# Turning transposed sums back to rows on GpSimd instead of ScalarE, with earlier row and weight loads, in a transformer block kernel

## The chip, the core and the metric

The kernel runs on one core of a Trainium2 chip. Its time is the device time of one execution in microseconds (us), and the median of several runs is given. A core has engines that work side by side, each through its own list of instructions in order: PE (TensorE, matrix products), DVE (VectorE), ACT (ScalarE), POOL (GpSimd) and SP (SyncE, which here only issues transfers). PEld is the weight load that belongs to a product and overlaps it. An instruction that waits for another engine or for a transfer holds up everything behind it in its own list.

## The reference, cut to what matters

One transformer block over 2048 rows of width 512, all in float32: a LayerNorm with scale and shift from a condition vector, attention of 32 heads (8 key and value heads, head size 128) over the last 512 cached keys, a gated residual, a second such LayerNorm, and a gated feed-forward part of width 1792 with its own gated residual.

```
mod = (silu(c) @ w_mod).reshape(1, 6, 1, 512);  sa, ca, ga, sb, cb, gb = mod
h = layernorm(x) * (1 + ca) + sa
x = x + ga * (softmax((h @ wq) @ k[-512:].T / sqrt(128)) @ v[-512:] @ wo)     # per head, k and v shared by 4 heads
h = layernorm(x) * (1 + cb) + sb
out = x + gb * ((gelu(h @ w_gate) * (h @ w_up)) @ w_down)
```

## The kernel before, in words

**Products.** Every float32 matrix is split into a high and a low float16 half, and `mm3` (line 90) makes each product out of three matmuls of 128x128 by 128x512 that accumulate in PSUM. A square of blocks is multiplied with seven block products instead of eight (`PROD`, numbered 1 to 7, with sums of blocks as operands); the partial results sit in chains named a, b and c.

**Stages.** The attention fills about the first 1340 us; its order is written out by hand for all engines. Then comes the feed-forward part, which the change touches. It is a loop over q = 0 to 27, with seven steps k = 0 to 6 in each, one block product per step. q counts pairs: n = q // 2 is a pair of 128-wide slices of the feed-forward width (seven pairs, `NP` = 7), and q even is the gate product, q odd the up product. The seven pairs are run twice, for the two halves g = 0 and g = 1 of the rows (n = 0 to 6 and n = 7 to 13). For g = 1 the LayerNorm rows must be prepared during g = 0: `ln_turned` loads a row tile, normalizes it on ACT (line 539), splits it into halves `xh` (lines 543 and 544) and has it transposed by a DMA (`xt`, line 549); `turned_out` (lines 558 and 559) makes scaled float32 tiles `hf`, which go to DRAM; `combos` loads them again (`cb`) and makes the block sums.

**Down product.** For the first five pairs of each half (`turned(n)`), the product with w_down is made transposed with the seven-product scheme. `yt_add` (lines 1657 and 1660) gathers it on DVE in eight tiles `yt`, one for each c of four column blocks and qb of two groups of 512 rows. For the last two pairs (`NROW` = 2) the product is made directly as rows, `y_tasks` (line 952), and added to the row tiles `acc`, eight of them for a half. After the fifth pair the eight `yt` tiles are turned back to rows, in four steps. `yt_turn` splits the 32-bit words of a tile into two 16-bit halves (`yu`, line 1666, on ACT); a DMA transposes them as 16-bit data (`yv`, line 1671, issued by SP); the rows of y1, the residual, are loaded into `acc` (`load_acc`, line 96); and `yt_row` puts the two halves together again for one row tile (`yr`, line 1686, on ACT, which reads pairs of 16-bit values that lie 1 KB apart) and adds the result to `acc` (line 1687, on POOL). `f_final` writes a row tile to the output when its three contributions are in.

**Order.** In the feed-forward part the list of SP is in program order; those of PE, ACT, DVE and POOL are arranged by a planner that goes by estimated readiness. `f_at(q, k, fn)` puts a step at a place of the loop, `put_off(n, fn)` puts it n steps on. `wd_fetch` fetches row weights `wo`, `set_fetch` the gate and up weights `w` and `x`. Tiles share buffers by tag: `qt` has 3, `v16` 2, `raw` 5, `acc` 8, and `rw` and `wr` 2 each, which only the preparation of weights uses, earlier on.

Of the kernel before, what the change touches and what calls it, by code (L numbers as in the profile page):

```python
# [22 lines left out]
KT = D // P  # L23
NF = F // P
NT = S // P
QB = 512
QT = QB // P
# [18 lines left out]
NRW = 2  # L46
NWR = 2
NROW = 2
# [16 lines left out]
def block_kernel(ctx: ExitStack, tc: tile.TileContext, x, kT, v, wq, wo, wg, wu, wd, cT, wc, wm, out):  # L65
    nc = tc.nc

    const = ctx.enter_context(tc.tile_pool(name="const", bufs=1))
    pool = ctx.enter_context(tc.tile_pool(name="pool", bufs=2))
# [7 lines left out]
    def raw(name):  # L77
        return pool.tile([P, 512], F32, tag="raw", name=name, bufs=NRAW)
# [13 lines left out]
    acc, moved, bg = {}, [0], []  # L92

    def dma(out_, in_):
        moved[0] += 1
        nc.sync.dma_start(out_, in_)

    def load_acc(i, src, eng=None):
        acc[i] = pool.tile([P, D], F32, tag="acc", name="acc", bufs=2 * QT)
        (eng.dma_start if eng else dma)(acc[i], src)  # L100

    def rows_of(t, i):
        return t[i * P:(i + 1) * P, :]
# [3 lines left out]
    for i in range(QT):  # L107
        load_acc(i, rows_of(x, i), nc.scalar if i < 2 else None)
# [184 lines left out]
    def turned(n):  # L293

        return n % NP < NP - NROW
# [59 lines left out]
    BK, hs, y1 = {}, {}, {}  # L355

    def spilled(gen, key):
        if (gen, key) not in hs:
            n = KT if key in (0, 1) else 2
            hs[gen, key] = dram.tile([P, n, QB], F32, name=f"hs{gen}_{key}")  # L360
        return hs[gen, key]
# [94 lines left out]
    def put_off(n, fn):  # L456

        waits_.append([n, fn])
# [70 lines left out]
    def ln_turned(i):  # L529

        qb, i_ = divmod(i, QT)
        st = {}

        def load():
            st["x"] = raw("xs")
            dma(st["x"], y1[2 * QT + i])

        def norm():
            nc.scalar.activation(st["x"], st["x"], AF.Identity, bias=col("kinv", i), scale=col("kmax", i))

        def split():
            st["p"] = t = pool.tile([P, 2, W], F16, tag="p16", name="xh", bufs=NP16)
            nc.scalar.activation(t[:, 0, :], st["x"], AF.Copy)
            nc.gpsimd.tensor_tensor(t[:, 1, :], st["x"], t[:, 0, :], op=ALU.subtract)

        def turn():
            if i_ == 0:
                TURN[qb] = pool.tile([P, QT, 2 * KT, P], F16, tag="pt", name="xt", bufs=NPT)
            nc.sync.dma_start_transpose(TURN[qb][:, i_], st["p"].rearrange("p a b -> p (a b)"))

        return load, norm, split, turn

    def turned_out(qb, dt):
        tag, n = (("qt", 3), ("v16", 2))[dt % 2]
        f = pool.tile([P, D], F32, tag=tag, name="hf", bufs=n)
        v = f.rearrange("p (t q) -> p t q", t=QT)
        sc = cols[:, 4, dt:dt + 1]
        nc.scalar.activation(v, TURN[qb][:, :, dt, :], AF.Identity, scale=sc, bias=cols[:, 3, dt:dt + 1])
        nc.vector.scalar_tensor_tensor(v, TURN[qb][:, :, KT + dt, :], sc, v, op0=ALU.mult, op1=ALU.add)
        put_off(3, lambda: dma(spilled(3, qb)[:, dt, :], f))  # L560
# [170 lines left out]
    def at(key, *fns):  # L731
        later.setdefault(key, []).extend(fns)
# [300 lines left out]
    for i in range(QT, 2 * QT):  # L1033
        load_acc(i, rows_of(x, i))
# [175 lines left out]
    for g in range(NG):  # L1210
# [9 lines left out]
        elif g >= GW and (not half or pr < GW):  # L1220
            sched_set(g, srcs, t0, by, spread)
            if not half:
                a, b, c, d, e, f = SETPOS2 if g == GW else SETPOS
# [28 lines left out]
    NP = NF // 2  # L1252
# [283 lines left out]
    with tc.manual_schedule():  # L1536
        begin()
        nexty, invs = [], {}
        for t in range(T + TAIL):
            now[0] = t  # L1540
            u, s = divmod(t, 4)
# [70 lines left out]
    def f_at(q, k, *fns):  # L1612
        at(("f", q, k), *fns)

    for n in range(1, 2 * NP):
        for k, at_ in ((0, 1), (2, 3), (1, 4), (3, 5)) if turned(n) else ((0, 1), (1, 4)):
            f_at(2 * n + 1, at_, lambda n=n, k=k: wd_fetch(n, k))
    for q in range(3, NQ):
        for k, at_ in ((0, 2), (3, 2), (1, 3), (2, 4)):
# [2 lines left out]
    def step(q, fn):  # L1622
        f_at(q // 7, q % 7, fn)

    for i in range(2 * QT):
        q = 7 * (2 + i // 2) + 3 * (i % 2)
        load, norm, split, turn = ln_turned(i)
        step(q - 4, load)
        step(q, norm)
        step(q + 1, split)  # L1630
        step(q + 3, turn)
    for k, (qb, dt) in enumerate(((0, 0), (0, 2), (0, 1), (0, 3), (1, 0), (1, 2), (1, 1), (1, 3))):
        step(31 + 2 * k if k < 4 else 39 + k, lambda qb=qb, dt=dt: turned_out(qb, dt))
    for p in range(2):
        q = 51 + 14 * p
        for load, steps in combos(3, p, nc.gpsimd):
            step(q - 2, load)
            for off, fn in steps:
                step(q + 2 * off, fn)

    def f_final(ti):
        assert ti in back
        halfway[ti] = halfway.get(ti, 0) + 1
        if halfway[ti] <= NROW:
            return
        if ti >= 2 * QT:
            dma(rows_of(out, ti), acc[ti])
        else:
            put_off(2, lambda: dma(rows_of(out, ti), acc[ti]))

    YT, YR, back, halfway = {}, {}, set(), {}

    def yt_add(n, c, qb, ps):
        by = ST["dyc"][:, KT * (n % NP) + c:KT * (n % NP) + c + 1]
# [3 lines left out]
        else:  # L1658
            YT[key] = pool.tile([P, QB], F32, tag="acc", name="yt", bufs=2 * QT)
            nc.vector.tensor_scalar(YT[key], ps, by, None, op0=ALU.mult)  # L1660

    def yt_turn(g, c, qb):

        def split():
            u = YR["u", c, qb] = pool.tile([P, 2, QB], U16, tag="qt", name="yu", bufs=3)
            nc.scalar.activation(u, YT[g, c, qb].bitcast(U16).rearrange("p (r h) -> p h r", h=2), AF.Copy)

        def turn():
            if ("t", qb) not in YR:
                YR["t", qb] = pool.tile([P, KT, 2 * QT, P], U16, tag="pt", name="yv", bufs=NPT)  # L1670
            nc.sync.dma_start_transpose(YR["t", qb][:, c], YR.pop(("u", c, qb)).rearrange("p a b -> p (a b)"))

        split()
        put_off(3, turn)
        YR["n"] = YR.get("n", 0) + 1
        if YR["n"] % QT == 0:
            for i in range(QT):
                ti = 2 * QT * g + (YR["n"] - 1) % (2 * QT) // QT * QT + i
                put_off(3, lambda ti=ti: load_acc(ti, y1[ti]) or back.add(ti))

    def yt_row(g, qb, i):
        t = YR["t", qb].rearrange("p c (h i) q -> p c q h i", h=2)
        ti = 2 * QT * g + QT * qb + i
        assert ti in back
        r = raw("yr")
        nc.scalar.activation(r.bitcast(U16).rearrange("p (c q h) -> p c q h", c=KT, h=2), t[:, :, :, :, i], AF.Copy)
        nc.gpsimd.tensor_tensor(acc[ti], acc[ti], r, op=ALU.add)
        f_final(ti)
        if i == QT - 1:
            del YR["t", qb]  # L1690

    ADDS = {1: ((0, 0),), 2: ((0, 0),), 6: ((0, 1),), 5: ((1, 1),), 7: ((1, 1),), 4: ((1, 0),), 3: ((0, 1),)}
    YORDER = (1, 2, 6, 5, 7, 3, 4)
    LAST = {2: (0, 0), 7: (1, 1), 3: (0, 1), 4: (1, 0)}

    def yt_tasks(n):
        tasks = []
        for p in range(2):
            st = {}
            bk = banks(st, {"a": ("acc", "ya", NACC) if p else ("qa", "ya", 1), "b": ("acc", "yb", NACC), "c": ("acc", "yc", NACC)})  # L1700

            def group(k, p=p, bk=bk):
                a, b = PROD[k]
                x, start = CHAIN[k]
                ci, off = YCOL[a]
                w, t = WO["f", n, ci], A[n, {"b11": "11", "b21": "21", "b22": "22"}.get(b, b)]
                sl = slice(off + p * P, off + (p + 1) * P)
                mm3(bk(x)(), w[:, 0, sl], w[:, 1, sl], t[:, 0, :], t[:, 1, :], start, k in (2, 4, 3), True)

            def post(k, p=p, st=st):  # L1710
                (i, qb), = ADDS[k]
                yt_add(n, 2 * i + p, qb, st[CHAIN[k][0]])
                if n % NP == NP - NROW - 1 and k in LAST:
                    i, qb = LAST[k]
                    c, g = 2 * i + p, n // NP
                    put_off(2 if k in (3, 4) and p == k // 4 else 1, lambda: yt_turn(g, c, qb))
                    if p and k in (3, 4):
                        for r in range(QT):
                            put_off((9 if k == 4 else 13) + r, lambda r=r: yt_row(g, qb, r))

            tasks += [(lambda k=k, f=group: f(k), lambda k=k, f=post: f(k)) for k in YORDER]
        return [tasks[k:k + 2] for k in range(0, len(tasks), 2)]

    YCOL = {"a11": (0, 0), "a12": (0, 256), "s2": (1, 0), "s3": (1, 256), "s4": (2, 0), "s1": (2, 256), "a22": (3, 0)}
# [2 lines left out]
    for q in range(NQ):  # L1727
        n, m = divmod(q, 2)
# [55 lines left out]
```

## Time and profile before

| | |
|---|---|
| median of 3 runs | 1743.84 us (1743.32 to 1745.21) |
| the profiled execution's own time | 1743.57 us |
| its span, first to last instruction | 1741.8 us |
| PE busy | 1714.7 us, 98% |
| DVE busy | 1417.6 us, 81% |
| ACT busy | 1258.5 us, 72% |
| POOL busy | 1045.9 us, 60% |
| granted TensorE clock | 1.000 |

The profile's times count from the first instruction. PE's busy time counts the modelled end of each matmul, so a steady stream of matmuls shows as fully busy; how many were issued in a stretch tells more. A row of the timeline gives the start, the duration, the engine, line and operation, and in square brackets the idle time of the engine ahead of it with what ended it. A q behind an engine's name means its issuing part alone.

### The profile page before, as it was taken

How to read it: one execution, taken by the hardware profiler on the slowest of the kernel's cores; microseconds unless marked ns; L12 is line 12 of the kernel's file. 1: busy time of each engine (PE TensorE's matmuls, PEld its weight loads, DVE VectorE, ACT ScalarE, POOL GpSimd, SP SyncE). 2: the span in 40 equal slices, each digit the busy share in tenths (PEclk: the TensorE clock that was granted, in tenths of full speed). 3: DMA queues.
4: the chain of work that ended last, by engine and by line, in shares of the span. 5: the costliest groups of instructions: out<-in, count | busy, mean ns of one | idle time of the engine just before them, and what ended most of it. 6: DMA issues, size and time to landing. Idle time of an engine off the chain costs nothing.

```text
span 1741.8 us, 26188 instructions
## 1 busy us (share of the span) xinstructions
PE 1714.7 (98%) x8022; PEld 787.0 (45%) x8022; DVE 1417.6 (81%) x2454; ACT 1258.5 (72%) x2813; POOL 1045.9 (60%) x1266
## 2 busy tenths in 40 slices
PE   7999999999999999999999999999999999999998
PEld 5444444444444444444444444444444444444443
DVE  7898898888888899888888788888886678556674
ACT  6988788888878777898778778787784554643344
POOL 4889778776788884654675665754621558313422
PEclk9999999999999999999999999999999999999999
DMA  7999999999999999999999999899986663743235
GB/s 236 218 205 211 213 214 207 223 206 221 215 217 228 205 205 187 212 213 230 201 219 224 208 223 220 186 235 218 197 180 150 187 177 128 191 139 100 91 97 167
DMA packets 690636, 339.82 MB, mean 195 GB/s; under 512 B 578880, under 2 KB 601408, under 8 KB 690496
## 3 DMA queue, kind: packets, MB, share of 16 engines
q1 hardware_dynamic: 690208, 337.63, 85.5%
q8 instruction: 63, 1.03, 0.3%
q14 instruction: 77, 0.63, 0.1%
q10 hardware_dynamic: 288, 0.52, 0.1%
HBM read 135.66 MB, written 61.87 MB: 113 GB/s over the span
## 4 chain that ended last, share of the span: by engine, by line
PE 82%; ACT 5%; DVE 5%; DMA 3%; POOL 2%; issue 2%; SPq 0%; ACTq 0%; DVEq 0%; POOLq 0%
PE py L90 19%; PE ps L90 17%; PE po L90 17%; PE qa L90 8%; PE fa L90 6%; PE qc L90 4%; PE fc L90 3%; PE ya L90 2%; PE qb L90 2%; PE fb L90 2%; PE yc L90 1%; ACT ee L991 1%; DMA yv<-yu 1%; ACT p L1003 1%; DVE nm L982 1%
## 5 line engine op out<-in xcount | busy, mean ns | idle before, releaser
L991 ACT ACTIVATE ee<-ps,nm 128x512 f32<-128x512 f32 x512 | 350.1, 684 | 191.9 <-DVE nm L982 189.3
L1008 DVE SCALAR_TENSOR_TENSOR p<-ee,rr,p 128x512 f16<-128x512 f32 x512 | 460.0, 898 | 4.5 <-ACT p L1003 3.9
L982 DVE TENSOR_REDUCE nm<-ps 128x1 f32<-128x512 f32 x512 | 350.4, 684 | 106.1 <-PE ps L90 103.2
L90 PE MATMUL ps<-k,qt 128*128 128x512 f16 x1536 | 414.9, 379 | 5.6 <-ACT ee L991 4.4
L1003 ACT ACTIVATE p<-ee,rr 128x512 f16<-128x512 f32 x512 | 364.6, 712 | 19.0 <-DVE rr L999 10.0
L90 PE MATMUL po<-pt,v 128*128 128x512 f16 x1536 | 373.0, 379 | 2.7 <-DVE kmax L183 1.4
L90 PE MATMUL py<-wo,ot 128*128 128x512 f16 x1536 | 371.5, 379 | 0.1
L90 PEld LDWEIGHTS <-w 128*128 128x128 f16 x2184 | 213.3, 98 | 263.3 <-issue 4.7
L90 PEld LDWEIGHTS <-v 128*128 128x128 f16 x1536 | 149.9, 98 | 184.9 <-DMA pt<-p 2.3
L90 PEld LDWEIGHTS <-ot 128*128 128x128 f16 x1536 | 150.3, 98 | 181.7 <-DVE ot L740 0.5
L90 PEld LDWEIGHTS <-qt 128*128 128x128 f16 x1536 | 145.9, 98 | 176.9 <-issue 4.7
L1303 POOL TENSOR_TENSOR fg<-fg 128x512 f32<-128x512 f32 x40 | 51.8, 1295 | 135.6 <-DVE fg L1287 103.0
L740 DVE SCALAR_TENSOR_TENSOR ot<-po,ot 128x512 f16<-128x512 f32 x128 | 87.7, 685 | 39.1 <-ACT ot L739 38.6
L1297 ACT ACTIVATE at<-fg 128x512 f16<-128x512 f32 x86 | 53.4, 625 | 64.8 <-DVE fg L1287 44.5
L991 ACT ACTIVATION_READ_ACCUMULATOR ee<-ps,nm 128x1 f32 x512 | 99.9, 195 | 0.0
L952 DVE SCALAR_TENSOR_TENSOR acc<-py,ysc,acc 128x512 f32<-128x512 f32 x128 | 94.7, 740 | 6.2 <-PE py L90 6.2
L235 POOL TENSOR_TENSOR lw<-lw,half__86 128x1 f32<-128x1 f32 x37 | 23.4, 633 | 104.2 <-DVE lw L185 104.1
L90 PE MATMUL fa<-t,w 128*128 128x512 f16 x336 | 83.6, 379 | 1.9 <-ACT u L885 1.4
L90 PE MATMUL qa<-t,w 128*128 128x512 f16 x348 | 84.9, 379 | 0.0
L397 POOL TENSOR_TENSOR rs<-rs,nhalf 128x1 f32<-128x1 f32 x32 | 18.8, 586 | 103.6 <-DVE rs L391 100.7
L739 ACT ACTIVATE ot<-po 128x512 f16<-128x512 f32 x128 | 73.8, 577 | 5.0 <-PE po L90 5.0
L1657 DVE SCALAR_TENSOR_TENSOR yt<-ya,dyc,yt 128x512 f32<-128x512 f32 x68 | 50.1, 745 | 22.1 <-PE ya L90 21.7
(241 smaller groups left out, 2794.0 us busy)
## 6 DMA issues: line engine op xcount, KB each, us to landing
w<-kept SPq DMA_DIRECT2D x123, 256.0 KB, 3.3
wo<-kept SPq DMA_DIRECT2D x70, 256.0 KB, 3.4
kept<-stage SPq DMA_DIRECT2D x61, 256.0 KB, 3.3
raw<-in_wo SPq DMA_DIRECT2D x56, 256.0 KB, 3.2
kept<-w SPq DMA_DIRECT2D x39, 256.0 KB, 3.4
rw<-in_wq SPq DMA_DIRECT2D x38, 256.0 KB, 3.2
hs<-hf SPq DMA_DIRECT2D x32, 256.0 KB, 2.9
pt<-p SPq DMA_TRANSPOSE x512, 3.5
```

The lines of the kernel that those rows point to most:

```text
L90: nc.tensor.matmul(ps, a, b, start=first and n == 0, stop=last and n == 2, skip_group_check=chain)
L235: nc.gpsimd.tensor_tensor(out, out, half_, op=ALU.pow)
L739: nc.scalar.activation(t[:, 0, :], src, AF.Copy, scale=scale)
L740: return lambda: nc.vector.scalar_tensor_tensor(t[:, 1, :], src, scale, t[:, 0, :], op0=ALU.mult, op1=ALU.subtract)
L952: nc.vector.scalar_tensor_tensor(acc[ti], st["p"], by, acc[ti], op0=ALU.mult, op1=ALU.add)
L982: nc.vector.tensor_reduce(nm, E[t]["ps"], axis=AX.X, op=ALU.max, negate=True)
L991: nc.scalar.activation(e, E[t]["ps"], AF.Exp, bias=E[t]["nm"], scale=1.0, accum_out=sm[:, t % 2:t % 2 + 1])
L1003: nc.scalar.activation(p16[:, 0, :], E[t]["e"], AF.Copy, scale=E[t]["r"])
L1008: nc.vector.scalar_tensor_tensor(p16[:, 1, :], E[t]["e"], E[t]["r"], p16[:, 0, :], op0=ALU.mult, op1=ALU.subtract)
L1297: nc.scalar.activation(t[:, 0, :], g, AF.Copy)
L1303: nc.gpsimd.tensor_tensor(g[o], g[a], g[b], op=ALU.subtract)
L1657: nc.vector.scalar_tensor_tensor(YT[key], ps, by, YT[key], op0=ALU.mult, op1=ALU.add)
```

## The change

- `yu` and `yr` are made by POOL with a copy instead of ACT. `yu` takes its buffers in turn from `qt` and `v16`, five in all instead of three.
- The addition of `yr` to `acc` is put by `whole` only behind the first direct addition of DVE to that row tile; `f_final` and `halfway` follow from it.
- The row tiles of the first row group of each half are loaded before q = 10 and q = 24 begin, into `rw` and `wr`; those of the second group four steps after the fourth `yt_turn`, into `acc`.
- In the second half of the columns (p = 1) the block products 3 and 4 change places, so that the first row group is complete first. The steps of `yt_row` come 7 or 8 steps on instead of 9 or 13, two in a step.
- The row weights of the pairs that are not turned are fetched at steps 0 and 1 instead of 1 and 4.
- In the preparation of the LayerNorm, the issue of the transposing DMA, `turned_out` and `combos` move two steps on.

```diff
-    def load_acc(i, src, eng=None):
-        acc[i] = pool.tile([P, D], F32, tag="acc", name="acc", bufs=2 * QT)
+    def load_acc(i, src, eng=None, tag="acc", bufs=2 * QT):
+        acc[i] = pool.tile([P, D], F32, tag=tag, name="acc", bufs=bufs)
...
-        for k, at_ in ((0, 1), (2, 3), (1, 4), (3, 5)) if turned(n) else ((0, 1), (1, 4)):
+        for k, at_ in ((0, 1), (2, 3), (1, 4), (3, 5)) if turned(n) else ((0, 0), (1, 1)):
             f_at(2 * n + 1, at_, lambda n=n, k=k: wd_fetch(n, k))
...
-        step(q + 3, turn)
+        step(q + 5, turn)
...
-        step(31 + 2 * k if k < 4 else 39 + k, lambda qb=qb, dt=dt: turned_out(qb, dt))
+        step(33 + 2 * k if k < 4 else 41 + k, lambda qb=qb, dt=dt: turned_out(qb, dt))
     for p in range(2):
-        q = 51 + 14 * p
+        q = 53 + 14 * p
...
+    def whole(ti):
+        if ti in halfway and ti in joined:
+            nc.gpsimd.tensor_tensor(acc[ti], acc[ti], joined[ti], op=ALU.add)
+
     def f_final(ti):
         assert ti in back
         halfway[ti] = halfway.get(ti, 0) + 1
-        if halfway[ti] <= NROW:
+        if halfway[ti] == 1:
+            return whole(ti)
+        if halfway[ti] < NROW:
             return
+        assert ti in joined
...
+    def rows_in(g, qb, tags):
+        for i in range(QT):
+            ti = 2 * QT * g + QT * qb + i
+            load_acc(ti, y1[ti], None, *tags[i // 2])
+            back.add(ti)
+
+    for g in range(2):
+        f_at(2 * (NP * g + NP - NROW) - 1, 6, lambda g=g: rows_in(g, 0, (("rw", NRW), ("wr", NWR))))
...
-            u = YR["u", c, qb] = pool.tile([P, 2, QB], U16, tag="qt", name="yu", bufs=3)
-            nc.scalar.activation(u, YT[g, c, qb].bitcast(U16).rearrange("p (r h) -> p h r", h=2), AF.Copy)
+            tag, bufs = (("qt", 3), ("v16", 2))[YR.get("n", 0) % 2]
+            u = YR["u", c, qb] = pool.tile([P, 2, QB], U16, tag=tag, name="yu", bufs=bufs)
+            nc.gpsimd.tensor_copy(u, YT[g, c, qb].bitcast(U16).rearrange("p (r h) -> p h r", h=2))
...
-        if YR["n"] % QT == 0:
-            for i in range(QT):
-                ti = 2 * QT * g + (YR["n"] - 1) % (2 * QT) // QT * QT + i
-                put_off(3, lambda ti=ti: load_acc(ti, y1[ti]) or back.add(ti))
+        if YR["n"] % (2 * QT) == QT:
+            put_off(4, lambda: rows_in(g, 1, (("acc", 2 * QT),) * 2))
...
-        nc.scalar.activation(r.bitcast(U16).rearrange("p (c q h) -> p c q h", c=KT, h=2), t[:, :, :, :, i], AF.Copy)
-        nc.gpsimd.tensor_tensor(acc[ti], acc[ti], r, op=ALU.add)
-        f_final(ti)
+        nc.gpsimd.tensor_copy(r.bitcast(U16).rearrange("p (c q h) -> p c q h", c=KT, h=2), t[:, :, :, :, i])
+        joined[ti] = r
+        whole(ti)
...
-    YORDER = (1, 2, 6, 5, 7, 3, 4)
+    YORDER = ((1, 2, 6, 5, 7, 3, 4), (1, 2, 6, 5, 7, 4, 3))
...
-                    put_off(2 if k in (3, 4) and p == k // 4 else 1, lambda: yt_turn(g, c, qb))
+                    put_off(2 if k == 3 else 1, lambda: yt_turn(g, c, qb))
                     if p and k in (3, 4):
                         for r in range(QT):
-                            put_off((9 if k == 4 else 13) + r, lambda r=r: yt_row(g, qb, r))
+                            put_off((7 if k == 4 else 8) + r // 2, lambda r=r: yt_row(g, qb, r))
```

More of the change, by code (lines that the diff above doesn't have):

```diff
@@ L1649, in f_final @@
             put_off(2, lambda: dma(rows_of(out, ti), acc[ti]))
-    YT, YR, back, halfway = {}, {}, set(), {}
+    YT, YR, back, halfway, joined = {}, {}, set(), {}, {}
     def yt_add(n, c, qb, ps):
@@ L1715, in post @@
                     c, g = 2 * i + p, n // NP
-                    put_off(2 if k in (3, 4) and p == k // 4 else 1, lambda: yt_turn(g, c, qb))
+                    put_off(2 if k == 3 else 1, lambda: yt_turn(g, c, qb))
                     if p and k in (3, 4):
                         for r in range(QT):
-                            put_off((9 if k == 4 else 13) + r, lambda r=r: yt_row(g, qb, r))
-            tasks += [(lambda k=k, f=group: f(k), lambda k=k, f=post: f(k)) for k in YORDER]
+                            put_off((7 if k == 4 else 8) + r // 2, lambda r=r: yt_row(g, qb, r))
+            tasks += [(lambda k=k, f=group: f(k), lambda k=k, f=post: f(k)) for k in YORDER[p]]
         return [tasks[k:k + 2] for k in range(0, len(tasks), 2)]
```

## The prediction

> **What bounds the kernel now.** I read the page's engine shares and the chain that ended last, then stage windows, then the engines' timelines near the end.
>
> ```profile
> span 1741.8 us, 26188 instructions
> PE 1714.7 (98%) x8022; PEld 787.0 (45%) x8022; DVE 1417.6 (81%) x2454; ACT 1258.5 (72%) x2813; POOL 1045.9 (60%) x1266
> PE 82%; ACT 5%; DVE 5%; DMA 3%; POOL 2%; issue 2%; SPq 0%; ACTq 0%; DVEq 0%; POOLq 0%
> ```
>
> PE is the bound, and the change alters none of its work, so it can only give back what PE loses in the feed-forward part. The windows tell how much that is (x counts the matmuls issued):
>
> ```profile
> core 0: us, PE busy (x) PEld busy (x) DVE busy (x) ACT busy (x) POOL busy (x), PEclk, DMA share, GB/s
> 1375.00:1402.00 27.00, 25.57 (x116) 11.14 (x115) 22.52 (x30) 18.47 (x32) 17.26 (x14) 1.00 0.75 200
> 1402.00:1510.00 108.00, 107.23 (x496) 48.30 (x494) 82.98 (x116) 53.78 (x89) 60.23 (x49) 1.00 0.51 150
> 1510.00:1550.00 40.00, 39.61 (x183) 17.71 (x182) 19.30 (x29) 21.73 (x30) 9.96 (x8) 1.00 0.56 164
> 1550.00:1700.00 150.00, 150.00 (x697) 67.99 (x695) 101.23 (x149) 59.55 (x98) 48.24 (x40) 1.00 0.36 110
> 1700.00:1737.76 37.76, 34.72 (x154) 14.37 (x151) 19.68 (x29) 18.73 (x23) 10.30 (x8) 1.00 0.58 164
> ```
>
> From 1550 to 1700 PE issues 697 in 150 us, 4.65 per us (0.215 us each), and waits for nothing. By that rate it lost 9.5 matmuls (2.0 us) in the first row, 5.9 (1.3 us) in the second, 2.9 (0.6 us) in the third and 21.5 (4.6 us) in the last. These 8.5 us are the whole prize, 0.5%. The waits of the last row, and what ACT did then:
>
> ```profile
> 1713.59 1.47 PE L90 MATMUL fc<-t,w 128*128 128x512 f16 x6 [0.86 <-DMA w<-kept]
> 1724.09 1.46 PE L90 MATMUL fa<-t,w 128*128 128x512 f16 x6 [0.74 <-ACT u L885]
> 1726.23 1.46 PE L90 MATMUL fa<-t,x 128*128 128x512 f16 x6 [0.69 <-ACT u L885]
> 1698.69 2.94 ACT L1666 ACTIVATE yu<-yt 128x1024 uint16<-128x1024 uint16 x3
> 1714.42 5.43 ACT L1686 ACTIVATE yr<-yv 128x1024 uint16<-128x1024 uint16 x5 [3.21 <-DMA yv<-yu]
> 1720.27 3.29 ACT L1686 ACTIVATE yr<-yv 128x1024 uint16<-128x1024 uint16 x3
> 1715.67 10.30 POOL L1687 TENSOR_TENSOR acc<-acc,yr 128x512 f32<-128x512 f32 x8 [32.52 <-ACT yr L1686]
> 1735.28 3.34 DVE L952 SCALAR_TENSOR_TENSOR acc<-py,dysc,acc 128x512 f32<-128x512 f32 x4 [0.54 <-PE py L90]
> ```
>
> ACT's copies stand in its list ahead of the evacuations `u` that PE needs: 8.7 us of `yr`, begun late because ACT waited 3.2 us for a transposition. POOL, idle 32.5 us before, was done by 1726, and DVE's last addition, at 1738.62, waited for PE only.
>
> **POOL's copies in the change.** Sixteen `yu` (u each) and sixteen `yr` (r each) leave ACT and join POOL, eight and eight per half. No row shows a POOL copy of 1024 16-bit values. The nearest:
>
> ```profile
> L158 POOL TENSOR_SCALAR w<-rw 128x512 f16<-128x512 f32 x50 | 42.0, 840 | 3.5
> L158 POOL TENSOR_SCALAR x<-rw 128x256 f16<-128x256 f32 x16 | 10.5, 656 | 1.4
> L1303 POOL TENSOR_TENSOR fg<-fg 128x512 f32<-128x512 f32 x40 | 51.8, 1295 | 135.6 <-DVE fg L1287 103.0 <-ACT fg L1276 31.9
> L798 POOL TENSOR_TENSOR rw<-rw 128x256 f32<-128x256 f32 x64 | 55.7, 870 | 4.3
> L239 POOL TENSOR_SCALAR acc<-acc,mv,rs 128x512 f32<-128x512 f32 x8 | 17.9, 2240 | 0.0
> ```
>
> One operand costs 0.184 us per 256 elements more, 0.72 ns each, so 1024 take 0.84 + 512 x 0.00072 = 1.21 us; doubling 0.84 gives 1.68. Below 0.84 I exclude: twice the elements of that row. Above, the dearest row, 2240 ns for 512, would give 4.5 us. I take 1.4 for both copies, between the two readings of the row they are nearest to.
>
> [...]
>
> **The end, limited by POOL.** SP issues the eight transpositions (the fourth is the second of the x2 row) and the loads between them:
>
> ```profile
> 1697.71 0.75 DVE L1657 SCALAR_TENSOR_TENSOR yt<-ya,dyc,yt 128x512 f32<-128x512 f32 x1
> 1696.27 4.72 SPq L1671 DMA_TRANSPOSE yv<-yu  x2
> 1701.09 1.95 SPq L96 DMA_DIRECT2D acc<-y  x4
> 1707.78 1.23 SPq L1671 DMA_TRANSPOSE yv<-yu  x1
> 1709.06 0.58 SPq L96 DMA_DIRECT2D w<-kept  x1
> 1711.02 2.53 SPq L96 DMA_DIRECT2D acc<-y  x4
> 1713.59 0.91 SPq L96 DMA_DIRECT2D wo<-kept  x2
> DMA to landing us min/median/max: 3.1/3.9/5.2
> ```
>
> The fourth was issued at 1696.27 + 4.72 - 1.23 = 1699.76, as soon as ACT had turned the sum that DVE finished at 1698.46. From there SP issues one after another without a pause. In the changed program the list from the fourth to the eighth transposition holds the same items (the one group of four row loads in it is now that of the second row group), but that sum comes four matmuls later, 0.9 us, at about 1699.3. So the fourth goes out at 1699.3 + 1.4 = 1700.7, 0.9 us later than before, and all behind it too, the gate and up weights included. The seventh now completes the first row group: 1707.78 + 0.9 + 5.2 (longest landing, the queue being dense) = 1713.9. POOL's list is then five `yr`, five additions, three `yr`, three additions: 8 x 1.4 + 10.30 = 21.5 us, to 1735.4. DVE's last addition (3.34 / 4, about 0.8) ends at 1736.2. Before, it ended 3.2 us ahead of the span's end, so the span is 1739.4, plus 8 (r - 1.4) + (u - 1.4).
>
> **The end, limited by PE.** Without ACT's copies nothing stands ahead of the two `u` or the last `at`. What stays is the lateness of weights: PE already waited 0.86 us for the fetch issued at 1709.06, and fetches now go 0.9 later; some PE work also moved ahead of it. I leave 0.9 of the 4.6 us: a span of 1741.8 - 3.7 = 1738.1. POOL's 1739.4 is later and counts: 2.4 us gained at the end.
>
> **The rest of the change.** The second group's loads (2.5 us of SP) no longer stand ahead of the two `wo`, which PE wants only for the final rows; DVE's waits for `acc` go with them; no PE row above names one, so nothing. The first group's four loads move on SP ahead of the first transposition, into buffers long free: 4 x 0.49 us of issue, hidden behind what SP has fetched ahead, else 2.0. The first `yu` now stands among POOL's sums of the fifth pair, which ended at 1715.67 - 32.52 = 1683.15, and puts the last of them off by 1.4 us; its product feeds the addition of 1697.71, so it is hidden, else 1.4. The eighth `yu` waits for the fourth landing, 1700.7 + 5.2 = 1705.9, and is done by 1707.3, ahead of SP, which reaches it near 1710.6. In the first half the same POOL chain has room:
>
> ```profile
> 1542.16 2.73 DVE L952 SCALAR_TENSOR_TENSOR acc<-py,dysc,acc 128x512 f32<-128x512 f32 x4 [1.91 <-PE py L90]
> 1562.91 2.62 POOL L1303 TENSOR_TENSOR fg<-fg 128x512 f32<-128x512 f32 x2 [31.89 <-ACT fg L1276]
> SPq L549 <- POOL xh L544: 5.6, 3, 4.2
> ACT hf L558 <- DMA xt<-xh: 8.7, 2, 6.9
> PE ya L90 <- DMA w<-kept: 0.8, 1, 0.8
> ```
>
> POOL sat idle 31.9 us until 1562.91, and the final additions begin at 1542.16. So ACT's copies there leave for nothing, and of the 0.6 us of 1510 to 1550 I take 0.5. The LayerNorm transpositions, two steps on, are what the other rows price: SP stood 5.6 us for `xh` with weight fetches queued behind (PE waited 0.8 for one), and ACT stood 8.7 us for `xt`. `turned_out` moves by the same two steps, so ACT's wait shrinks only as far as `xt` was late for SP's sake. I take half of 2.0, and 0.3 of the 1.3 of 1402 to 1510, where `combos` falls on other sums. Together 1.8 us; the bounds are 3.9, all of it, and a loss of 2.0, the same trouble once more in a new place.
>
> **Sum.** 1739.4 - 1.8 = 1737.6 of span. The execution took 1743.57, 1.77 above its span: 1739.4 us. The median of the runs is 0.27 above that execution, which I leave out. 0.2% (3.5 us) is about what a measurement of this kernel can tell from no change; the forecast, 4.4 under the median, is just beyond it.
>
> **Rivals.**
> 1. POOL becomes the bound, slower. Place: `yr`, whose neighbouring values lie 1 KB apart. A further operand costs POOL (1.295 - 0.870) / 256 - 0.00072 = 0.94 ns per element; if each strided value costs two such accesses more, r = 1.21 + 1024 x 0.00188 = 3.1, though overlap should save some: I take 2.9. Then 1739.4 + 8 x 1.5 = 1751.4 us. It decides from r = 2.4 on (1747.4). For it: nothing hides POOL there. Against: ACT's `yr` costs hardly more than its `yu`. [...]
> 2. One access more, r = 1.21 + 0.96 = 2.2: 1745.8 us, no change. ACT's gain is handed to POOL.
> 3. The copies are cheap, but the moved LayerNorm steps give nothing and lose 2.0 elsewhere: 1739.4 + 3.8 = 1743.2, no change. For it: DVE is at 81% and the planner has rearranged PE, DVE and ACT from the gate product of the second pair on.
> 4. Slower `yu` too: at u = 2.9 the transpositions go 1.5 us later still and PE waits that much for weights, with r = 2.4: 1739.4 + 8 + 1.5 = 1748.9, slower.
>
> **Chances.** The forecast 0.42; rival 1 0.22; rival 2 0.17; rival 3 0.12; rival 4 0.07. So faster 0.42, same 0.29, slower 0.29. The forecast's own range is 1735 (PE limits at r = 1.2, all 3.9 and the 0.9 left at the end regained: 1737.2 - 3.9 + 1.8 = 1735.1) to 1742 (r = 1.7: 1739.4 + 2.4). The whole range goes to 1751, rival 1.
>
> **What would show it.** `yr` on POOL near 1.4 us and `yu` the same; ACT free of both; PE's waits for `u` after 1720 gone, one for `w` of about 0.9 left; the last POOL addition near 1733.6 (1735.4 - 1.8) and DVE's last addition waiting for it and not for PE; fewer lost matmuls between 1375 and 1402, with no SP wait for `xh`. The prediction is wrong if `yr` takes over 2.4 us, if `yu` holds up SP, or if new PE waits arise before 1550.

## The result and the profile after

The changed kernel takes 1748.55 us (median of 10 runs, 1747.07 to 1750.29) against 1744.38 us for the kernel before on the same chip (1743.32 to 1745.49): ratio 1.0023, 95% interval 1.0014 to 1.0032. It became slower by 4.2 us where 4.4 us of gain were forecast. The profiled execution took 1750.29 us, with a span of 1748.5 us, and is one of the longer ones.

The span, the engines' shares and the chain that ended last, from the page of the changed kernel:

```profile
span 1748.5 us, 26169 instructions
PE 1717.0 (98%) x8020; PEld 787.3 (45%) x8022; DVE 1425.4 (82%) x2454; ACT 1228.4 (70%) x2781; POOL 1085.5 (62%) x1298
PE 84%; DVE 5%; ACT 4%; POOL 3%; DMA 2%; issue 1%; SPq 1%; DVEq 0%; POOLq 0%; ACTq 0%
```

ACT gave up 30.1 us and POOL took on 39.6 us; PE is still the bound. The windows of the changed kernel, the last one cut where its PE ends, as in the prediction (x counts the matmuls issued):

```profile
1375.00:1402.00 27.00, 25.72 (x118) 11.41 (x117) 23.86 (x29) 19.64 (x33) 19.37 (x16) 1.00 0.72 193
1402.00:1510.00 108.00, 103.92 (x480) 46.51 (x477) 83.27 (x115) 46.32 (x78) 64.15 (x52) 1.00 0.46 141
1510.00:1550.00 40.00, 37.89 (x175) 17.05 (x176) 20.75 (x26) 11.15 (x18) 25.10 (x20) 1.00 0.63 161
1550.00:1700.00 150.00, 150.00 (x697) 67.92 (x695) 100.19 (x146) 57.47 (x94) 52.99 (x44) 1.00 0.38 119
1700.00:1744.38 44.38, 40.16 (x176) 17.02 (x173) 26.37 (x35) 8.15 (x13) 26.12 (x21) 0.96 0.53 133
```

At the same 4.65 matmuls per us as before, PE lost 7.5 matmuls in the first row (1.6 us), 22.2 in the second (4.8), 11.0 in the third (2.4) and 30.4 in the last (6.5). Before, these were 2.0, 1.3, 0.6 and 4.6. So 4.9 us were lost ahead of 1550, and the end, which was to give back 2.4, lost 1.9 more. The 6.8 us together are the difference of the two spans, 6.7.

PE's waits behind this, from the timeline of the changed kernel:

```profile
1452.93 0.59 PE L90 MATMUL yc<-at,wo 128*128 128x512 f16 x2 [0.62 <-ACT at L1297]
1480.86 1.46 PE L90 MATMUL fa<-t,w 128*128 128x512 f16 x6 [0.57 <-ACT fg L885]
1484.27 0.59 PE L90 MATMUL yc<-at,wo 128*128 128x512 f16 x2 [1.95 <-ACT at L1297]
1510.49 1.47 PE L90 MATMUL fa<-t,w 128*128 128x512 f16 x6 [1.42 <-DMA w<-kept]
1520.06 1.47 PE L90 MATMUL fa<-b,w 128*128 128x512 f16 x6 [1.62 <-DMA w<-kept]
1715.43 2.46 PE L90 MATMUL fa<-b,w 128*128 128x512 f16 x6 [2.24 <-DMA w<-kept]
1717.68 2.20 PE L90 MATMUL fb<-b,w 128*128 128x512 f16 x6
1734.90 2.76 PE L90 MATMUL py<-wo,at 128*128 128x512 f16 x12 [0.78 <-ACT at L1297]
1738.45 0.61 PE L90 MATMUL py<-wo,at 128*128 128x512 f16 x2 [0.78 <-ACT at L1297]
1739.46 4.92 PE L90 MATMUL py<-wo,at 128*128 128x512 f16 x22 [0.41 <-DVE at L1298]
```

There are three families: gate products (`at`, `fg`) that come late from 1452 to 1484, weights `w` that come late, and gate products that come late in the last 10 us. Counted from start to start of the matmuls, they cost 3.6 us (0.8 + 0.7 + 2.1), 5.8 us (1.6 + 1.8 + 2.4) and 2.5 us (0.94 + 0.95 + 0.57). The waits for `u`, 1.75 us before, are gone. The twelve matmuls from 1715.43 on took 4.28 us instead of some 2.6, because the granted clock was 0.50 for 3.4 us (1715.8 to 1719.2) behind that wait.

The new work on POOL is cheap, as the groups of the changed kernel show:

```profile
L1643 POOL TENSOR_TENSOR acc<-acc,yr 128x512 f32<-128x512 f32 x16 | 23.4, 1491 | 0.0
L1701 POOL COPY yr<-yv 128x1024 uint16<-128x1024 uint16 x16 | 20.0, 1294 | 19.6 <-DMA yv<-yu 19.6
L1683 POOL COPY yu<-yt 128x1024 uint16<-128x1024 uint16 x16 | 17.2, 1098 | 29.0 <-DVE yt L1664 26.5 <-DMA yv<-yu 2.5
```

### The profile page after: what moved, and what is told of

Read it like the earlier page. It is cut to its first block, busy times and chain, and to the rows that moved or that the text cites. A ratio compares the mean times of both kernels' runs of the same rounds, so it can differ in the third digit from the quotient of the medians.

```text
span 1748.5 us, 26169 instructions
## 1 busy us (share of the span) xinstructions
PE 1717.0 (98%) x8020; PEld 787.3 (45%) x8022; DVE 1425.4 (82%) x2454; ACT 1228.4 (70%) x2781; POOL 1085.5 (62%) x1298
## 4 chain that ended last, share of the span: by engine, by line
PE 84%; DVE 5%; ACT 4%; POOL 3%; DMA 2%; issue 1%; SPq 1%; DVEq 0%; POOLq 0%; ACTq 0%
PE py L90 19%; PE ps L90 17%; PE po L90 17%; PE qa L90 8%; PE fa L90 7%; PE qc L90 4%; PE fc L90 3%; PE ya L90 2%; PE qb L90 2%; PE fb L90 2%; PE yc L90 1%; PE pq L90 1%; ACT ee L991 1%; ACT p L1003 1%; DVE nm L982 1%
## 5 line engine op out<-in xcount | busy, mean ns | idle before, releaser
L159 POOL TENSOR_TENSOR stage<-rw,stage 128x512 f16<-128x512 f32 (+1 forms) x56 | 64.7, 1155 | 4.7
```

Of the source, the lines that this page charges most:

```text
L159: nc.gpsimd.tensor_tensor(dst[:, 1, :], src, dst[:, 0, :], op=ALU.subtract)
```

## Experiments

The causes that the trace suggests were numbered as follows, and the expectations use these names. Theory 1: the moved LayerNorm steps put `combos` on POOL ahead of the gate sums. Theory 2: the copies on POOL make SP wait for `yu`, with weight fetches queued behind. Theory 3: any new order costs something somewhere. Theory M: POOL's work at the end slows DVE. Each time stands beside runs of the kernel before on the same chip.

**Undoing the LayerNorm moves.** `a_ln_back` is the changed kernel with the old steps; `b_ln_only` is the kernel before with the new ones.

```diff
-        step(q + 5, turn)
+        step(q + 3, turn)
-        step(33 + 2 * k if k < 4 else 41 + k, lambda qb=qb, dt=dt: turned_out(qb, dt))
+        step(31 + 2 * k if k < 4 else 39 + k, lambda qb=qb, dt=dt: turned_out(qb, dt))
-        q = 53 + 14 * p
+        q = 51 + 14 * p
```

> The changed kernel, but the LayerNorm's transpositions, turned_out and combos stand at their old steps (two earlier). Theory 1 (the moved steps put combos' work on POOL ahead of the fifth pair's gate sums, and PE waits for these): PE's waits at 1452, 1480 and 1484 (0.8 + 0.7 + 2.1 us, 3.6 together) go, PE issues about 495 matmuls from 1402 to 1510 instead of 480, the waits for weights near 1510 and 1520 stay; 3.6 us less than the changed kernel, near 1745, ratio to before 1.000 to 1.001. Theory 2 (POOL's copies and the row order did it): nothing gained, 1748 to 1749, with the same loss between 1402 and 1510. Theory 3 (any new order of the planner costs something, wherever it is made): a loss of 2 to 4 us at other places, 1747 to 1749.

> The kernel before, with nothing but the LayerNorm's transpositions, turned_out and combos two steps later. Theory 1: it loses the same 3.6 us between 1402 and 1510, near 1748, ratio 1.002, with all of before's waits in the tail unchanged. Theory 2: no loss, 1743 to 1744.5, as the copies stay on ACT. Theory 3: 1746 to 1748, with the waits of PE at other places than in the changed kernel.

`a_ln_back` took 1743.70 us against 1744.14 (ratio 0.9998, 0.9990 to 1.0007): the whole loss is gone. Two windows of it:

```profile
1402.00:1510.00 108.00, 107.14 (x496) 48.37 (x495) 82.95 (x117) 46.61 (x80) 69.41 (x57) 1.00 0.52 155
1510.00:1550.00 40.00, 39.90 (x186) 18.02 (x184) 21.87 (x30) 12.53 (x20) 20.45 (x16) 1.00 0.54 153
```

The 496 matmuls of before are back. So are those of the next row (186), where the expectation had let the two waits for weights stay: they went too. `b_ln_only` took 1745.92 us (ratio 1.0011, 1.0002 to 1.0019), slower by 1.8 us and not by 3.6; its profile has the waits for `at` near 1452 and 1482 and one of 1.6 us for `w` near 1514. Theory 1 holds. The moved steps cost more inside the change (4.6 us, from 4.2 above the kernel before to 0.4 below it) than alone (1.8 us); which other part of the change makes the difference was not told apart.

**Which of the three moves.** `a_combos_back` undoes the last line of the diff above alone, `a_turns_back` the first two.

> The changed kernel, with the two combos alone at their old steps (two earlier); the transpositions and turned_out stay two steps later. Theory 1a (combos' own steps put POOL's b, cb and t work ahead of the gate sums): the 3.6 us of PE's waits for the gate products between 1450 and 1485 go, near 1744 to 1745. Theory 1b (the later transpositions deliver hf later, and combos and what follows come late whatever their steps): the waits stay or grow, since combos would now wait for data that is two steps late, 1748 or more.

> The changed kernel, with the LayerNorm's transpositions and turned_out at their old steps; the two combos stay two steps later. Theory 1a: the waits between 1450 and 1485 stay at about 3.6 us, 1747.5 to 1748.5; of what lies between 1388 and 1402 (1.8 us in the changed kernel) up to 1 us may change. Theory 1b: the waits go, near 1744 to 1745.

`a_combos_back` took 1744.20 us against 1744.68 (ratio 1.0000, 0.9991 to 1.0009), `a_turns_back` 1748.54 us (1.0025, 1.0015 to 1.0036). It is the step of `combos`; moving the transpositions and `turned_out` makes no difference that these intervals show. POOL's timeline shows the mechanism, first in the changed kernel (with the last gate product that DVE delivers for the gate sums):

```profile
1467.65 1.16 POOL L378 TENSOR_TENSOR b<-cb,b 128x512 f16<-128x512 f32 x1 [4.60 <-ACT b L374]
...
1479.24 0.96 DVE L1287 SCALAR_TENSOR_TENSOR fg<-fg,gsc,u 128x512 f32<-128x512 f32 x1
1479.62 2.72 POOL L378 TENSOR_TENSOR t<-cb,t 128x512 f16<-128x512 f32 x2
1482.29 2.61 POOL L1303 TENSOR_TENSOR fg<-fg 128x512 f32<-128x512 f32 x2
```

and then in `a_combos_back`:

```profile
1470.51 2.71 POOL L378 TENSOR_TENSOR t<-cb,t 128x512 f16<-128x512 f32 x2
1478.47 2.63 POOL L1303 TENSOR_TENSOR fg<-fg 128x512 f32<-128x512 f32 x2 [5.25 <-DVE fg L1287]
```

With the old step POOL has finished the block sums by 1473.2, sits idle 5.25 us, and makes the gate sums as soon as DVE delivers them. Two steps later the same sums fill POOL almost without a gap from 1467.65 to 1482.3, and the gate sums queue behind them. DVE has delivered by 1480.20 and POOL begins at 1482.29, 2.1 us late; PE's wait, which ends at 1484.27, is 2.1 us.

**One copy back on ACT.** `a_yu_act` and `a_yr_act` return one of the two copies each.

```diff
-            nc.gpsimd.tensor_copy(u, YT[g, c, qb].bitcast(U16).rearrange("p (r h) -> p h r", h=2))
+            nc.scalar.activation(u, YT[g, c, qb].bitcast(U16).rearrange("p (r h) -> p h r", h=2), AF.Copy)
```

```diff
-        nc.gpsimd.tensor_copy(r.bitcast(U16).rearrange("p (c q h) -> p c q h", c=KT, h=2), t[:, :, :, :, i])
+        nc.scalar.activation(r.bitcast(U16).rearrange("p (c q h) -> p c q h", c=KT, h=2), t[:, :, :, :, i], AF.Copy)
```

> The changed kernel, with the sixteen yu copies on ACT again (yr stays on POOL). Theory 2 for yu (the copies wait in POOL's list, SP waits for them with weight fetches queued behind, and PE waits for these): SP's waits ahead of the second transposition (12.4 us near 1500, 11.5 us near 1700) shrink to under 5, PE's waits for w at 1510, 1520 and 1713 (1.6 + 1.8 + 2.4 us) and the half clock after the last of them (1.7 us in half of the runs) go: 4 to 6 us less, 1743 to 1745. Theory 1: the 3.6 us between 1402 and 1510 stay; only what it finds beside them can go, 1746 to 1747. If SP only moves its waits to another place: 1748, no gain.

> The changed kernel, with the sixteen yr copies on ACT again (yu stays on POOL). If POOL's long list of yr copies and additions at the end disturbs DVE's last products (they stretch from 0.75 to 1.4 us while POOL adds) and sets the end: PE's waits after 1730 (0.9 + 0.9 + 0.6 us) go, 1 to 2 us less, near 1747. If ACT's copies stand ahead of the evacuations u again, as in the kernel before: PE's waits for u (0.7 + 0.7 us) come back and the sum is near 1748.5, no change. Theory 1 and theory 2 (for yu) both leave the losses ahead of 1720 as they are.

`a_yu_act` took 1747.46 us (ratio 1.0022, 1.0012 to 1.0033) and `a_yr_act` 1748.56 us (1.0023, 1.0014 to 1.0033). Theory 2 in this form falls: with `yu` on ACT, SP's longest wait for it after 1670 is still 8.5 us instead of 11.5, where under 5 was expected, so the copies on POOL account for 3 us of it at most. PE still waits 2.0 us for `w` at 1709, and 2.6 us for `at` at 1731. With `yr` on ACT, the waits of the last 10 us shrink from 2.5 to 0.8 us and PE does not wait for `u` again, as theory M has it, but a wait of 2.65 us for `w` at 1709.8 and six slow matmuls behind it (2.74 us instead of 1.47) take the gain away.

**POOL beside DVE at the end.** On top of `a_ln_back`, `a_ln_back_yr_g1` gives the `yr` copies of the second half to ACT, and `a_ln_back_no_add` leaves POOL's additions of that half out.

```diff
-        nc.gpsimd.tensor_copy(r.bitcast(U16).rearrange("p (c q h) -> p c q h", c=KT, h=2), t[:, :, :, :, i])
+        (nc.gpsimd.tensor_copy if g == 0 else nc.scalar.copy)(r.bitcast(U16).rearrange("p (c q h) -> p c q h", c=KT, h=2), t[:, :, :, :, i])
```

```diff
-        if ti in halfway and ti in joined:
+        if ti in halfway and ti in joined and ti < 2 * QT:
```

> The changed kernel with all LayerNorm steps back, and the eight yr copies of the second half on ACT again (yu stays on POOL). Theory M (POOL's work beside it stretches DVE's last gate products, and PE waits 0.96 + 1.07 + 0.46 us for at): these waits shrink to about 0.8, as in the run with all yr on ACT, and PE does not wait for u as it did in the kernel before, as ACT now stands free of yu: 1.5 us less than with the LayerNorm steps back alone, 1742.2, ratio to before 0.999. Rival (ACT's copies stand ahead of u again): PE waits 0.7 + 0.7 us for u, 1743.7, nothing gained.

> The changed kernel with all LayerNorm steps back, in which POOL leaves out the additions of yr to acc in the second half (the output then lacks these terms); its yr copies stay. It measures what POOL's additions cost DVE. Theory M, additions alone: DVE's last products take 0.75 instead of up to 1.5 us, PE's waits for at after 1727 go from 2.5 to about 0.8, 1742. If the yr copies stretch DVE's products as the additions do, they still do so beside the copies, which come to lie in the same stretch: 1743 to 1744. If nothing of DVE's stretching is due to POOL: the waits stay, 1743.7.

`a_ln_back_yr_g1` took 1742.47 us against 1744.68 (ratio 0.9986, 0.9977 to 0.9995), near the 1742.2 expected and faster than the kernel before; in its profile, the longest of its executions, PE's waits for `at` are down to the 0.8 us of theory M, beside a wait of 2.5 us for `w` at 1713. `a_ln_back_no_add` took 1743.10 us (0.9990, 0.9982 to 0.9999); its waits for `at` fell from 2.5 to 1.0 us, near the 0.8 expected, but with a wait of 2.1 us for `w` near 1709 it is 1.1 us over the 1742 expected. DVE's last gate products in the changed kernel, which run beside POOL's last additions and copies, with two instructions among them that read one operand from PSUM (`py`, `fa`):

```profile
1729.04 0.75 DVE L952 SCALAR_TENSOR_TENSOR acc<-py,dysc,acc 128x512 f32<-128x512 f32 x1 [1.84 <-PE py L90]
1730.42 1.43 DVE L1287 SCALAR_TENSOR_TENSOR fg<-fg,gsc,u 128x512 f32<-128x512 f32 x1
1732.55 0.98 DVE L1298 TENSOR_TENSOR at<-fg,at 128x512 f16<-128x512 f32 x1 [0.70 <-ACT at L1297]
1733.45 0.73 DVE L1287 SCALAR_TENSOR_TENSOR fg<-fg,gsc,fa 128x512 f32<-128x512 f32 x1
1734.88 1.29 DVE L1298 TENSOR_TENSOR at<-fg,at 128x512 f16<-128x512 f32 x1 [0.70 <-ACT at L1297]
```

and the three gate products with both operands in SBUF in `a_ln_back_no_add`, where POOL has done its copies and is idle by then:

```profile
1722.57 0.75 DVE L1287 SCALAR_TENSOR_TENSOR fg<-fg,gsc,u 128x512 f32<-128x512 f32 x1
1724.01 0.69 DVE L1298 TENSOR_TENSOR at<-fg,at 128x512 f16<-128x512 f32 x1 [0.70 <-ACT at L1297]
1726.06 0.69 DVE L1298 TENSOR_TENSOR at<-fg,at 128x512 f16<-128x512 f32 x1 [0.69 <-ACT at L1297]
```

So 1.43, 0.98 and 1.29 us go back to 0.75, 0.69 and 0.69; in `a_ln_back`, which differs from this run by the additions alone, they are 1.45, 0.98 and 1.41. The cause is POOL's work beside them. The product at 1730.42 lies within POOL's additions (1726.35 to 1732.97) and the one at 1734.88 within its copies (1732.93 to 1737.19), so both kinds stretch DVE; which weighs more was not told apart. The three products that stretch, by 0.3 to 0.7 us, have both operands in SBUF. The two with an operand in PSUM, at 1729.04 and 1733.45, keep their 0.75 and 0.73 us beside the same work of POOL. In what way POOL holds up the three, the trace does not show.

**The weights: who issues, and in which order.** On top of `a_ln_back_yr_g1` and of `a_ln_back`, the row loads of the second row group were issued by ACT's queue, which frees 2.0 us of SP.

```diff
-            load_acc(ti, y1[ti], None, *tags[i // 2])
+            load_acc(ti, y1[ti], nc.scalar if qb else None, *tags[i // 2])
```

> The changed kernel with all LayerNorm steps back and the eight yr copies of the second half on ACT, and beside these the four row loads of each second row group issued by ACT's queue instead of SP's. Theory Q (the weights w of the last quarter are late because SP issues four row loads, 2.0 us, and transpositions, 1.2 us each, ahead of them): w is issued 2.0 us sooner, PE's wait for it near 1711 falls from 2.65 to 0.7 us, 1740.5, ratio 0.9975. Rival (the transfers themselves share the DMA engines, and it doesn't matter which queue issues first): the wait stays above 2 us, 1742.5, no gain.

> As the run before, with all copies on POOL. Theory Q: PE's wait for w falls by 1.5 us against the run with the LayerNorm steps back alone; PE's waits for at (2.5 us) stay: 1742.2. Rival: 1743.7.

The times are 1744.67 us (ratio 1.0001, 0.9992 to 1.0009) and 1744.50 us (0.9999, 0.9991 to 1.0008) against 1744.22: nothing gained, and the first has lost the 2.2 us that `a_ln_back_yr_g1` had gained on the kernel before. The fetch near 1711 came in time, but PE now waited for the one before it, 2.74 us at 1702.45 in the first of the two. Theory Q as put falls. Next, two fetches of each half were put ahead of the transposition for which SP stands longest.

```diff
-            f_at(q - 1, at_, lambda q=q, k=k: set_fetch(("f", q), ("f", q % (2 * NP)), k))
+            step(7 * (q - 1) + at_ - ({(2 * NP - 1, 0): 6, (2 * NP - 2, 2): 1}.get((q % (2 * NP), k), 0)), lambda q=q, k=k: set_fetch(("f", q), ("f", q % (2 * NP)), k))
```

> The changed kernel, with two weight fetches of each half (the last of one quarter, the first of the next) ahead of the second transposition of yu, for which SP stands 11.5 us, instead of behind it. Theory S (the weights are late because SP stands at a transposition with their fetches queued behind): PE's waits for w of 1.8 us near 1520 and 2.4 us near 1715 go or fall under 0.5, as does the half clock that follows the latter in half of the runs; the 3.6 us between 1450 and 1485 stay: 3 to 4 us less, 1745, ratio to before 1.0003. Rival (the transfers share the DMA engines and land late wherever they stand): 1748.

> The same with all LayerNorm steps back, all copies on POOL. Theory S: PE's wait for w of 1.6 us near 1710 goes and those for at (2.5 us) stay, 1742.2, ratio 0.9987. Rival: 1743.7.

> The same with the eight yr copies of the second half on ACT besides. Theory S: of the 3.4 us that PE lost after 1700 in the kernel without the early fetches, the 2.65 us for w go: 1740, ratio 0.9973, the fastest of all. Rival: 1742.5.

On the changed kernel this gave 1745.46 us against 1744.67 (ratio 1.0008, 0.9999 to 1.0017), 3.4 us better than the changed kernel, as expected in the sum; but its profile, the longest of its executions, has new waits for `w` of 2.2 and 1.2 us near 1524 and 1526 (from start to start), so the waits did not simply go. With the LayerNorm steps back it gave 1745.20 us (1.0000, 0.9992 to 1.0009), and with `yr` on ACT besides 1744.83 us (0.9998, 0.9989 to 1.0007): both expectations missed. SP's timeline in `a_ln_back_w_early` tells why:

```profile
1698.86 6.11 SPq L1688 DMA_TRANSPOSE yv<-yu  x3
1705.08 1.95 SPq L96 DMA_DIRECT2D acc<-y  x4
1707.07 1.23 SPq L1688 DMA_TRANSPOSE yv<-yu  x1
1708.40 0.62 SPq L96 DMA_DIRECT2D x<-kept  x1
1709.11 2.74 SPq L1688 DMA_TRANSPOSE yv<-yu  x1
1711.95 0.53 SPq L96 DMA_DIRECT2D w<-kept  x1
```

and in the timeline of its PE:

```profile
1715.02 2.74 PE L90 MATMUL fa<-t,w 128*128 128x512 f16 x6 [2.62 <-DMA w<-kept]
```

SP issues almost without a pause from 1698.86 on. The two fetches taken ahead are in time; the third, issued at 1711.95, is late, and it costs as much. The last variant takes the transpositions themselves out of SP's list.

```diff
-            nc.sync.dma_start_transpose(YR["t", qb][:, c], YR.pop(("u", c, qb)).rearrange("p a b -> p (a b)"))
+            nc.scalar.dma_start_transpose(YR["t", qb][:, c], YR.pop(("u", c, qb)).rearrange("p a b -> p (a b)"))
```

> The changed kernel with all LayerNorm steps back, in which ACT's queue issues the transpositions of the sums instead of SP's (all copies on POOL). Theory D (SP's list is dense from 1697 on, 18 us of issues, and PE waits for whichever fetch comes late in it): no wait of PE for w over 0.5 us after 1700; ACT gives 8 x 1.2 us to issuing and may hold u up by up to 1.7 us; PE's waits for at (2.5 us) stay: 1742 to 1744. Rival (the transfers make the weights late, whoever issues): a wait for w of 1.5 us or more stays, and the time is 1743.7 or more.

> The same, with the eight yr copies of the second half on ACT besides. Theory D: no wait for w over 0.5 us, the waits for at shrink to 0.8, but ACT's list now holds 9.6 us of transpositions and 8.7 us of copies ahead of u, as much as ever: 1741 to 1744. Rival: the wait for w stays, 1742.5 or more.

> The changed kernel with nothing but the transpositions of the sums issued by ACT's queue; the LayerNorm steps stay late. Theory D with theory 1a: PE's waits for w of 1.6, 1.8 and 2.4 us near 1510, 1520 and 1715 go, and the half clock behind the last with them, while the 3.6 us between 1450 and 1485 stay: 4 to 6 us less than the changed kernel, 1743 to 1744.5, ratio to before 0.999 to 1.000; the two losses then add up (2.6 us from SP's list and 4.9 us from the moved steps were measured one by one or beside each other). If the waits for w follow from the combos' lateness and not from SP's list: 1747 or more.

`a_ln_back_turn_act` took 1741.10 us against 1744.27 (ratio 0.9980, 0.9971 to 0.9988), the lowest time of all and 0.9 us under the range expected; with `yr` on ACT besides it is 1741.47 us (0.9982, 0.9973 to 0.9991), no better: PE still waits 1.86 us for `at` at 1728.25, where 0.8 was expected. Its SP, from the timeline:

```profile
1694.25 0.70 SPq L96 DMA_DIRECT2D w<-kept  x1
1695.04 0.70 SPq L96 DMA_DIRECT2D x<-kept  x1
1696.36 0.80 SPq L96 DMA_DIRECT2D w<-kept  x2
1698.16 0.86 SPq L96 DMA_DIRECT2D wo<-kept  x2
```

and all of its PE's waits after 1700:

```profile
1724.81 2.76 PE L90 MATMUL py<-wo,at 128*128 128x512 f16 x12 [1.19 <-ACT at L1297]
1728.47 0.61 PE L90 MATMUL py<-wo,at 128*128 128x512 f16 x2 [0.90 <-ACT at L1297]
1729.37 4.92 PE L90 MATMUL py<-wo,at 128*128 128x512 f16 x22 [0.29 <-DVE at L1298]
```

The last weights are issued by 1699, there is no wait for `w` left, and the waits for `at` stay, as theory D said. The transfers are no quicker: after 1695 `w` took 4.2 us (median of four) from issue to landing in the changed kernel and 4.6 (of two) here, so it is the earlier issue that helps. The edit takes out of SP's list both the issuing time of the transpositions and SP's waits for `yu` ahead of them (11.5 us near 1700); which of the two counts for more was not told apart. The changed kernel with this edit alone (`a_turn_act`) took 1744.55 us against 1744.63 (1.0002, 0.9993 to 1.0011), at the upper end of what was expected; its profile has no wait for `w` near 1510, 1520 or 1715. Each measured against the runs of the kernel before that stand beside it, the changed kernel improves by 4.3 us with this edit, by 4.6 with the LayerNorm steps back, and by 7.3 with both. That is 1.5 us less than the sum, no more than the intervals (about 1.6 us to either side of each) leave open; the late weights near 1510 and 1520, which either edit removes, would be counted in both.

In the profile of `a_ln_back_turn_act`, SP's last transposition, `xt`, starts at 1409.4 and ACT's first at 1488.2, so this run shows the transpositions of only one queue at a time.

**Two parts of the change alone.** `a_ln_back_yord_back` takes the order of the block products back as well; `b_pool_copies` is the kernel before with both copies on POOL.

```diff
-    YORDER = ((1, 2, 6, 5, 7, 3, 4), (1, 2, 6, 5, 7, 4, 3))
+    YORDER = ((1, 2, 6, 5, 7, 3, 4), (1, 2, 6, 5, 7, 3, 4))
-                    put_off(2 if k == 3 else 1, lambda: yt_turn(g, c, qb))
+                    put_off(2 if k in (3, 4) and p == k // 4 else 1, lambda: yt_turn(g, c, qb))
```

> The changed kernel with all LayerNorm steps back, and the order of the row products of before. Theory O (the sum that now comes four matmuls later puts off the fourth transposition and the weights behind it by about 0.9 us): PE's wait for w near 1710 is up to 0.9 us shorter than with the LayerNorm steps back alone, while the transposition that completes the first row group, and with it POOL's last list, may come 1.3 us later: 1743 to 1744. If the order counts for nothing: 1743.7 with the same waits.

> The kernel before, with both copies on POOL and nothing else changed. If freeing ACT is what gains: PE's waits for u near 1724 and 1726 (1.75 us) go, 1742.5 to 1743. Theory M (POOL's additions, now later, stretch DVE's last gate products): PE's waits for at grow from 0.7 to about 2.5 us, the same amount, and the time stays at 1744. With nothing of theory 1 in it, 1402 to 1510 keeps its 496 matmuls.

`a_ln_back_yord_back` took 1749.56 us against 1744.22 (ratio 1.0036, 1.0024 to 1.0049), 5.9 us more than `a_ln_back`, with executions from 1747.55 to 1759.90 us. Theory O is not borne out: beside the rest of the change the old order loses. The steps of `yt_row` stay as the change has them, 7 or 8 on instead of 9 or 13, so this does not say what the new order is worth by itself; old order and old steps together are the kernel before. In its profile PE loses 7.4 us after 1700 instead of 4.4, with waits for `w` at 1703, 1711.8 and 1716.6; and the stretch from DVE's last addition to the end of the span is 2 us longer (5.4 against 3.4 us), for a cause that stays open. `b_pool_copies` took 1744.96 us (0.9999, 0.9991 to 1.0008): moving the copies alone changes nothing. Of PE's waits for `u` one is left (0.7 us) and the waits for `at` are gone too, against theory M as put there, but PE waits 3.0 us for `wo` at 1702.1, and the eighteen matmuls behind that wait take 5.6 us instead of some 3.9.

## Why the prediction was wrong, by its own steps

**POOL's copies: right.** `yu` takes 1.10 us and `yr` 1.29 us; 1.4 was taken for both. Rivals 1, 2 and 4, which needed `yr` from 2.2 us on, fall with it. `yr`, which reads at steps of 1 KB, costs 18% more than `yu`. It is chance that the whole range, which reached to 1751 for rival 1's sake, holds the measured time.

**The end, limited by POOL: the list right, the bound wrong.** The eight `yr` and eight additions were put at 21.5 us and take 22.0 (6.47 + 6.62 + 4.26 + 4.61); it comes out so close because the copies are 0.5 us under their price and the additions 0.9 us over theirs. POOL's timeline of the changed kernel:

```profile
1719.93 6.47 POOL L1701 COPY yr<-yv 128x1024 uint16<-128x1024 uint16 x5 [9.81 <-DMA yv<-yu]
1726.35 6.62 POOL L1643 TENSOR_TENSOR acc<-acc,yr 128x512 f32<-128x512 f32 x5
1732.93 4.26 POOL L1701 COPY yr<-yv 128x1024 uint16<-128x1024 uint16 x3
1737.15 4.61 POOL L1643 TENSOR_TENSOR acc<-acc,yr 128x512 f32<-128x512 f32 x3
```

But they begin at 1719.9, not at 1713.9; 4.9 of these 6.0 us are what was lost ahead of 1550 beyond the loss of before. And DVE's last addition, from 1744.49 on, waits for PE, which is busy until 1744.4, and not for POOL, which is done at 1741.8. POOL decides through DVE's products, which it stretches, and not through its own end.

**The end, limited by PE: the failing step at the end is "I leave 0.9 of the 4.6 us".** It lost 6.5. That ACT no longer holds up `u` was right. The lateness of weights, priced at 0.9, was 2.4 us of wait in this execution and 1.7 us of half clock behind it; and DVE's stretching beside POOL, with 2.5 us of waits for `at`, was not in the sum at all. The fetch of `w` that PE waits for at 1715.43, in the kernel before and in the changed one:

```profile
1704.42 0.57 SPq L96 DMA_DIRECT2D w<-kept  x1
1710.61 0.84 SPq L96 DMA_DIRECT2D w<-kept  x1
```

Without these 4.9 us it goes out about 1.3 us later than before, and not 0.9, and PE reaches it about 0.6 us sooner (at 1713.0, against 1708.69 before). SP's list of transpositions and fetches, described in the prediction as "from there SP issues one after another without a pause", was the limit; only taking the transpositions out of it left no wait for `w` at all.

**The rest of the change: the failing step.** The prediction took "0.3 of the 1.3 of 1402 to 1510, where `combos` falls on other sums", 1.8 us of gain in all with "a loss of 2.0" as the far bound. The three rows lost 4.9 us more than before instead. It had looked at SP and ACT for the moved LayerNorm steps, not at what `combos` meets on POOL, where eleven sums and splits now stand right ahead of the gate sums that PE waits for. Undoing that one step brings 1744.20 us, undoing all three moves 1743.70. Rival 3 named the right part, with its loss too small (2.0), without the place, and as no change; the 0.29 given to slower went to rivals 1 and 4, which are wrong. One sign of being wrong that the prediction named did come: new PE waits before 1550.

**The order of the products** was priced at a delay of 0.9 us. Taken back alone it costs 5.9, but with steps of `yt_row` that belong to the new order, so the price of the order itself stays open.

## What to carry to other kernels

When a step is moved by a slot or two, look up what it meets on every engine it issues to: here 15 us of POOL work that had been done, among other sums, 5 us before the gate sums landed right in front of them, and the bound engine needed these next. When one fetch was late in SP's dense list, advancing it or freeing 2 us of issues only made another one late; what helped was taking the long issues (1.2 us and more each, with the waits ahead of them) out of the list. And work moved to POOL was not free for DVE, even where POOL had the time: the products with both operands in SBUF grew from 0.69 to 0.98 and 1.29 us, and from 0.75 to 1.43.

## What the runs showed that was not expected

- The granted clock was 0.50 for 3.4 us behind a wait of PE of 2.24 us in the changed kernel. Behind waits of 2.65 us in `a_yr_act` and 2.62 us in `a_ln_back_w_early`, the first six matmuls took 2.74 us instead of 1.47; behind 2.74 us in `a_ln_back_load_act_yr_g1` they took 1.47. So the length of the wait alone does not tell, in these runs, whether PE slows down. The changed kernel's ten runs lie in two groups, 1747.1 to 1748.0 us at a mean clock of 1.000 and 1749.1 to 1750.3 us at less, 2.1 us apart in the middle, which is near the 1.7 us that the twelve slow matmuls cost.
- A transposition takes its issuing queue 1.2 us when it goes through at once and up to 2.7 us in a dense list (1709.11 above), against 0.5 to 0.6 us for most of the weight fetches there.
- DVE's gate products stretch from 0.69 to as much as 1.29 us, and from 0.75 to 1.43, beside POOL's instructions, with no wait in the trace that names POOL.
